# RetNet attention then a gated feed-forward: one ordered load queue for the first chunk and the weights, and a new order around the first feed-forward stage

## The chip, the cores and the metric

The kernel runs on one core of one Trainium2 chip. The metric is the device time of one execution in microseconds (us); smaller is better. The kernel before takes 266.89 us (median of three runs, 266.13 to 267.51).

## The reference

The input is q, k and v of shape [4 batches, 8 heads, 768 positions, 64], and the weights of a feed-forward layer. A recurrent attention with a decay per head is followed by an RMS norm and a gated feed-forward layer:

```python
state = gamma * state + k[t] (outer) v[t]        # one 64x64 state for each batch and head
y[t]  = q[t] @ state / sqrt(64)                  # 768 steps
x     = y, heads side by side                    # 3072 tokens x 512
xn    = x / sqrt(mean(x * x) + 1e-6) * rms_g
out   = (silu(xn @ w_gate) * (xn @ w_val)) @ w_out   # 512 -> 1536 -> 512
```

All inputs and the output are float32; the kernel multiplies in bfloat16.

## The kernel before, in words

The 768 positions are cut into 6 chunks of 128. A chunk of all 4 batches makes 512 tokens, one feed-forward stage. This text calls the feed-forward stages F0 to F5, the batches b0 to b3, and writes q(0,3) for the q tile of chunk 0, batch 3.

Attention of a chunk and batch is done in pieces. `cast` (L138) makes bf16 copies of q and k and scales v by the decay into `vp`. `piece_t` (L158) transposes q and k on TensorE and ScalarE copies the result out of PSUM (L167). `piece_a` (L171) multiplies k and q and VectorE applies the causal mask (L181). `piece_y` (L186) forms y and, for the next chunk, the state update `kv`; VectorE scales y into x (L208), ScalarE sums its squares (L212), GpSimd makes the reciprocal root `rstd` (L230, L233), and ScalarE (chunk 0, L221 and L222) or VectorE and GpSimd (L224, L225) fold kv into the states `st_f` and `st_b`. `piece_n` (L236) normalizes x to xn, and `piece_x` (L248) brings xn transposed into xnT: in chunk 0 by TensorE and VectorE (L255, L256), in later chunks by a DMA transpose on the sync queue (L243).

A feed-forward stage (L278) has 12 slots `gv(n)`, each with 4 matmuls into `g_ps`, 4 into `v_ps`, a Silu on ScalarE (L292) and a product on VectorE (L293), and then 4 slots `down(b)` of 12 matmuls into `o_ps`, whose result ScalarE copies to `o_sb` (L301) and the sync queue stores (L302). The matmul results of the stages rotate through 4 PSUM buffers (`fps`), those of attention through 4 others (`aps`); `o_sb` has 3 buffers, the raw loads 8 of each name.

The order is written out by hand. Ahead of F0, chunk 0's attention runs in the order of a step list (L313). Then the pieces of chunk c+1 are put between the 16 slots of stage c (`PLAN`, `PLAN1` for chunk 1, L264 and L265). Each engine and each queue works in program order.

What is loaded when: at the start the sync queue takes the 12 tiles of chunk 0 (256 KB each, pieces of 256 bytes, float32). GpSimd's queue, which can convert while it moves, takes the gate and value weights in four blocks (`load_w`, W0 to W3, each two transfers) among the steps, and the three blocks of the output weights (`load_wo`, wo0 to wo2) right behind (L315). Chunk 1's loads stand behind the first four Silus of F0 (L328), the broadcast norm weight `g_bc` behind them (L330), and chunk 2's loads at slots 5, 7, 9 and 11 of F0 (L332). Six matmuls that compute nothing needed (`hot`, L319) run ahead of F0.

Of the kernel before, what the change touches and what calls it, by code (L numbers as in the profile page):

```python
# [17 lines left out]
def kernel(  # L18
# [51 lines left out]

    for b in range(B):
        load(0, b)


    ident = const.tile([128, 128], BF16, name="ident")
    make_identity(nc, ident)
    causal = const.tile([128, 128], BF16, name="causal")
    nc.gpsimd.memset(causal, 1.0)
    nc.gpsimd.affine_select(
        out=causal, in_=causal, compare_op=ALU.is_ge, fill=0.0, base=0,  # L80
        pattern=[[1, 128]], channel_multiplier=-1)

    pos_i = const.tile([128, NCH], mybir.dt.int32, name="pos_i")
    nc.gpsimd.iota(pos_i, pattern=[[C, NCH]], base=1, channel_multiplier=1)
    pos_f = const.tile([128, NCH], F32, name="pos_f")
    nc.gpsimd.tensor_copy(pos_f, pos_i)
    lnscale = const.tile([128, 1], F32, name="lnscale")
    nc.gpsimd.memset(lnscale, math.log(scale))
    zero = const.tile([128, 1], F32, name="zero")
    nc.gpsimd.memset(zero, 0.0)  # L90
    vdec = const.tile([128, NCH, H], F32, name="vdec")
    ydec = const.tile([128, NCH, H], F32, name="ydec")
    for h in range(H):
        nc.scalar.activation(vdec[:, :, h], pos_f, AF.Exp, scale=-lng[h], bias=zero)
        nc.scalar.activation(ydec[:, :, h], pos_f, AF.Exp, scale=lng[h], bias=lnscale)
    mhalf = const.tile([128, 1], F32, name="mhalf")
    nc.gpsimd.memset(mhalf, -0.5)

    warm = const.tile([128, 1], F32, name="warm")
    nc.scalar.activation(warm, zero, AF.Silu)  # L100
    g_col = const.tile([128, KS], F32, name="g_col")
# [11 lines left out]
    for b in range(B):  # L113
        nc.gpsimd.memset(st_b[b], 0.0)

# [7 lines left out]
    WB = 384  # L123

    def load_w(i):
        sl = slice(i * WB, (i + 1) * WB)
        nc.gpsimd.dma_start(out=wg_b[:, :, sl], in_=wg_v[:, :, sl])
        nc.gpsimd.dma_start(out=wv_b[:, :, sl], in_=wv_v[:, :, sl])

    def load_wo(i):  # L130
        sl = slice(i * 4, (i + 1) * 4)
        nc.gpsimd.dma_start(out=wo_b[:, sl, :], in_=wo_v[:, sl, :])


    cur = {}
    mark = {}

    def cast(c, b):  # L138
        q_f, k_f, v_f = raw.pop((c, b))
        qb = work.tile([128, DM], BF16, name="qb", bufs=6)  # L140
        kb = work.tile([128, DM], BF16, name="kb", bufs=6)
        vp = work.tile([128, H, D], BF16, name="vp", bufs=6)
        if c == 0:
            nc.vector.tensor_copy(qb, q_f.rearrange("p h d -> p (h d)"))
        else:
            nc.gpsimd.tensor_copy(qb, q_f.rearrange("p h d -> p (h d)"))  # L146
# [39 lines left out]
    def piece_y(c, b):  # L186
# [14 lines left out]
        if c < NCH - 1:  # L201
            kv_ps = aps.tile([128, NHP, 128], F32, name="kv_ps", tag="at")
# [12 lines left out]
        piece_rstd(c, b)  # L215
        if c < NCH - 1:
            for i in range(2):
                r = slice(i * 64, i * 64 + 64)
                kv = kv_ps[r, :, i * 64:i * 64 + 64]
                if c == 0:  # L220
                    nc.scalar.copy(st_b[b][r, :, i * 64:i * 64 + 64], kv)  # L221
                    nc.scalar.copy(st_f[b][r], kv)  # L222
                else:
                    nc.vector.tensor_tensor(out=st_f[b][r], in0=st_f[b][r], in1=kv, op=ALU.add)  # L224
                    nc.gpsimd.tensor_copy(st_b[b][r, :, i * 64:i * 64 + 64], st_f[b][r])  # L225
        d["x"] = x

# [50 lines left out]
    def ffn(c):  # L278
# [4 lines left out]
        def gv(n):  # L283
# [81 lines left out]
```

## Time and profile before

| what | value |
|---|---|
| time, median of three runs | 266.89 us |
| the profiled execution, its own time | 266.61 us |
| its span, first to last instruction | 264.9 us |
| TensorE (PE) busy in the span | 231.2 us |
| VectorE (DVE), ScalarE (ACT), GpSimd (POOL) busy | 124.8, 91.0, 93.9 us |
| mean granted TensorE clock | 0.987 of full speed |
| HBM read, written | 28.58 MB, 6.29 MB |

The profile is that of one execution. A matmul's end is modelled and matmuls overlap, so a stage is best measured from the start of one group to the start of another. POOLq and SPq are the instructions by which GpSimd and the sync engine issue DMAs; q0 is the DMA queue of GpSimd, q1 that of the sync engine. "idle before <-releaser" in a row tells how long the engine stood idle and what ended it.

### The profile page before, as it was taken

To read this page: it belongs to the slowest core of one execution; us is meant where nothing else is said; L and a number is where in the kernel's file an instruction comes from. 1 tells how busy PE (TensorE), PEld (TensorE's weight loads), DVE (VectorE), ACT (ScalarE), POOL (GpSimd) and SP (SyncE) were. 2 spreads that over 40 slices of the span, in tenths; PEclk is the share of its full clock that TensorE was granted. 3 is DMA by queue.
4 is the path that set the end of the run, shared out by engine and by line. 5 is a ranking of instruction groups with operands and counts; after the bars stand their busy time and mean duration, and the time that the engine had idled before them with its cause. 6 is when DMAs were issued, how large, how long until landed. Compare 5 with 4: busy or idle time off the path is not lost.

```text
span 264.9 us, 4103 instructions
## 1 busy us (share of the span) xinstructions
PE 231.2 (87%) x1467; PEld 112.6 (42%) x1494; DVE 124.8 (47%) x208; ACT 91.0 (34%) x187; POOL 93.9 (35%) x177
## 2 busy tenths in 40 slices
PE   1557899996908999999998999999999999999994
PEld 1334344543403454444444444544444444444441
DVE  0547144546421588703689403898126674044400
ACT  8546132424311334314333223323232432333311
POOL 6698301556249022493032690222950111000000
PEclk9999999999986999999999999999999999999999
DMA  8999999999964597944599844599645101300022
GB/s 159 218 172 203 203 199 213 218 200 223 202 216 86 122 190 152 148 139 101 101 216 216 142 143 97 122 227 221 128 120 99 42 20 59 114 27 0 0 82 79
DMA packets 112628, 37.24 MB, mean 141 GB/s; under 512 B 103776, under 2 KB 109408, under 8 KB 112608
## 3 DMA queue, kind: packets, MB, share of 16 engines
q1 hardware_dynamic: 106768, 32.26, 60.5%
q0 software_dynamic: 5840, 4.72, 11.6%
q8 instruction: 12, 0.20, 0.3%
q14 instruction: 8, 0.07, 0.1%
HBM read 28.58 MB, written 6.29 MB: 132 GB/s over the span
## 4 chain that ended last, share of the span: by engine, by line
PE 59%; DVE 12%; DMA 11%; ACT 4%; POOL 4%; SPq 4%; issue 4%; DVEq 0%; ACTq 0%; POOLq 0%
PE o_ps L298 21%; PE g_ps L287 16%; PE v_ps L290 15%; DMA k_f<-in_k_dram 5%; SPq L64 4%; DVE hT L293 4%; DVE am L181 4%; ACT sg L292 2%; DVE xn L241 2%; DMA g_bc<-in_moe_rms_g_dram 2%; DMA v_f<-in_v_dram 2%; PE a_ps L177 2%; DVE x L208 2%; PE y_ps L194 1%; ACT xsq L212 1%
## 5 line engine op out<-in xcount | busy, mean ns | idle before, releaser
L293 DVE TENSOR_TENSOR hT<-sg,v_ps 128x512 bf16<-128x512 bf16 x72 | 49.4, 687 | 94.6 <-PE v_ps L290 83.4
L287 PE MATMUL g_ps<-xnT,wg_b 128*128 128x512 bf16 x275 | 75.2, 390 | 8.7 <-DMA xnT<-xn 7.5
L290 PE MATMUL v_ps<-xnT,wv_b 128*128 128x512 bf16 x282 | 75.2, 386 | 0.5
L292 ACT ACTIVATE sg<-g_ps 128x512 bf16<-128x512 f32 x72 | 42.8, 594 | 71.4 <-PE g_ps L287 68.3
L298 PE MATMUL o_ps<-wo_b,hT 128*128 128x512 bf16 x281 | 63.1, 379 | 0.5 <-issue 0.2
L290 PEld LDWEIGHTS <-wv_b 128*128 128x128 bf16 x288 | 28.6, 99 | 35.3 <-issue 2.2
L287 PEld LDWEIGHTS <-wg_b 128*128 128x128 bf16 x288 | 26.6, 100 | 38.2 <-issue 11.6
L298 PEld LDWEIGHTS <-hT 128*128 128x128 bf16 x288 | 27.8, 98 | 32.3
L230 POOL TENSOR_SCALAR ms<-ssq 128x1 f32<-128x1 f32 x24 | 4.6, 191 | 103.1 <-ACT xsq L212 102.9
L181 DVE TENSOR_TENSOR am<-a_ps,causal 128x512 bf16<-128x512 f32 x48 | 30.8, 683 | 4.5 <-PE a_ps L177 4.5
L212 ACT ACTIVATE xsq<-x 128x512 f32<-128x512 f32 x24 | 15.1, 630 | 45.8 <-DVE x L208 45.6
L301 ACT COPY o_sb<-o_ps 128x512 f32<-128x512 f32 x24 | 14.1, 586 | 44.8 <-PE o_ps L298 37.8
L148 POOL TENSOR_TENSOR vp<-v_f,vdec 128x512 bf16<-128x512 f32 x24 | 25.4, 1060 | 2.5 <-DMA v_f<-in_v_dram 2.4
L241 DVE SCALAR_TENSOR_TENSOR xn<-x,rstd,g_bc 128x512 bf16<-128x512 f32 x20 | 15.5, 776 | 9.9 <-POOL rstd L233 7.8
L208 DVE TENSOR_TENSOR x<-y_ps,ydec 128x512 f32<-128x512 f32 x24 | 16.4, 685 | 7.3 <-PE y_ps L194 5.0
L146 POOL CAST qb<-q_f 128x512 bf16<-128x512 f32 x20 | 12.2, 610 | 14.5 <-DMA q_f<-in_q_dram 14.1
L194 PE MATMUL y_ps<-vp,am 128*128 128x64 bf16 x192 | 13.1, 203 | 4.1 <-DVE am L181 4.0
L147 POOL CAST kb<-k_f 128x512 bf16<-128x512 f32 x24 | 14.7, 612 | 4.9 <-DMA k_f<-in_k_dram 4.9
L194 PEld LDWEIGHTS <-am 128*128 128x128 bf16 x192 | 9.4, 104 | 12.6 <-DVE am L181 11.1
L225 POOL CAST st_b<-st_f 64x256 bf16<-64x256 f32 x32 | 14.0, 439 | 0.9
L233 POOL TENSOR_TENSOR rstd<-ms,mhalf 128x1 f32<-128x1 f32 x24 | 13.2, 552 | 2.0
L224 DVE TENSOR_TENSOR st_f<-st_f,kv_ps 64x256 f32<-64x256 f32 x32 | 13.2, 413 | 0.5
(48 smaller groups left out, 109.2 us busy)
## 6 DMA issues: line engine op xcount, KB each, us to landing
q_f<-in_q_dram SPq DMA_DIRECT2D x24, 256.0 KB, 4.6
k_f<-in_k_dram SPq DMA_DIRECT2D x24, 256.0 KB, 4.9
v_f<-in_v_dram SPq DMA_DIRECT2D x24, 256.0 KB, 5.0
out_dram<-o_sb SPq DMA_DIRECT2D x24, 256.0 KB, 2.1
wg_b<-in_moe_w_gate_dram POOLq DMA_DIRECT2D x4, 384.0 KB, 8.6
wv_b<-in_moe_w_val_dram POOLq DMA_DIRECT2D x4, 384.0 KB, 9.5
wo_b<-in_moe_w_out_dram POOLq DMA_DIRECT2D x3, 512.0 KB, 13.8
xnT<-xn SPq DMA_TRANSPOSE x20, 2.4
```

The costliest lines, as they stand in the source:

```text
L147: nc.gpsimd.tensor_copy(kb, k_f.rearrange("p h d -> p (h d)"))
L148: nc.gpsimd.tensor_tensor(out=vp, in0=v_f, in1=vdec[:, c, :, None].to_broadcast([128, H, D]), op=ALU.mult)
L181: nc.vector.tensor_tensor(out=am[:, i], in0=a_ps[i], in1=causal[:, None, :].to_broadcast([128, NHP, 128]), op=ALU.mult)
L194: nc.tensor.matmul(y_ps[:, h, :], d["am"][:, i, hp, :], d["vp"][:, h, :], start=first, stop=last, skip_group_check=True)
L208: nc.vector.tensor_tensor(out=x, in0=y_ps, in1=ydec[:, c, :, None].to_broadcast([128, H, D]), op=ALU.mult)
L212: nc.scalar.activation(xsq, x.rearrange("p h d -> p (h d)"), AF.Square, accum_out=ssq)
L241: nc.vector.scalar_tensor_tensor(out=xn, in0=x, scalar=d["rstd"], in1=g_bc, op0=ALU.mult, op1=ALU.mult)
L287: nc.tensor.matmul(g_ps, wg_b[:, s, sl], xnT[:, s, :], start=s == 0, stop=s == KS - 1)
L290: nc.tensor.matmul(v_ps, wv_b[:, s, sl], xnT[:, s, :], start=s == 0, stop=s == KS - 1)
L292: mark[c, n] = nc.scalar.activation(sg, g_ps, AF.Silu)
L293: nc.vector.tensor_tensor(out=hT[:, n, :], in0=sg, in1=v_ps, op=ALU.mult)
L298: nc.tensor.matmul(o_ps, hT[:, n, b * C:(b + 1) * C], wo_b[:, n, :], start=n == 0, stop=n == NFF - 1)
```

## The change

- Chunk 0: the tiles of b0 still come by the sync queue. Those of b1 to b3 go into GpSimd's queue (`load0`), q and k converted to bf16 on the way, v as float32; the nine transfers stand ahead of the weights, with the identity and the causal mask made between them. b0's q is cast by VectorE and its k by ScalarE; VectorE scales v (`piece_v`). The decay tables are made by two activations instead of sixteen. `g_col` is loaded by ScalarE's queue.
- Chunk 0's xT of b0 to b2 is emptied by ScalarE in four activations each instead of by VectorE in one. The state copies to `st_f` come after the last steps, those to `st_b` go to GpSimd into slots 0 to 3 of F0; `kv` of chunk 0 is held in `fps`.
- Weights: W1 to W3 stand behind the rstd of b0, b1 and b2 on GpSimd. Output weights are issued at slots 9 and 12 of F0, behind the casts of chunk 1's b2 and b3.
- Chunk 1's loads wait until W1 has landed; chunk 2's loads stand at slot 16, behind g_bc, and wait until wo1 has landed.
- F0 gets 24 slots: `down` goes over all four batches in thirds of the output weights. Chunk 1's pieces are spread over all 24. Chunk 1's xn is transposed by TensorE as in chunk 0, no longer by DMA.

```diff
-    for b in range(B):
-        load(0, b)
+    def load0(b):
+        for name, src in (("qb", q), ("kb", k)):
+            x = work.tile([128, DM], BF16, name=name, bufs=6)
+            nc.gpsimd.dma_start(
+                out=x.rearrange("p (h d) -> p h d", h=H),
+                in_=src[b].rearrange("h (c p) d -> c p h d", p=C)[0])
+            raw0[name, b] = x
+        x = loads.tile([128, H, D], F32, name="v_f")
+        nc.gpsimd.dma_start(out=x, in_=v[b].rearrange("h (c p) d -> c p h d", p=C)[0])
+        raw0["v", b] = x
+    load(0, 0)
...
+    load0(1)
     ident = const.tile([128, 128], BF16, name="ident")
     make_identity(nc, ident)
+    load0(2)
     causal = const.tile([128, 128], BF16, name="causal")
...
+    load0(3)
...
-            for i in range(2):
...
+    def piece_s(b):
+        for i in range(2):
+            r = slice(i * 64, i * 64 + 64)
+            nc.scalar.copy(st_f[b][r], cur[0, b]["kv"][r, :, i * 64:i * 64 + 64])
+    def piece_sb(b):
+        for i in range(2):
+            r = slice(i * 64, i * 64 + 64)
+            nc.gpsimd.tensor_copy(st_b[b][r, :, i * 64:i * 64 + 64], st_f[b][r])
...
+        if c == 0 and b < B - 1:
+            for s in range(KS):
+                nc.scalar.activation(cur[c, "xnT"][:, s, b * C:(b + 1) * C], xt_ps[:, s, :],
+                                     AF.Copy, scale=g_col[:, s:s + 1])
+            return
...
-    PLAN1 = dict(cast=(5, 7, 9, 11), t=(7, 9, 11, 13), a=(8, 10, 12, 14), y=(9, 11, 13, 15), n=(11, 13, 15, 15), x=(13, 15, 15, 15))
+    PLAN1 = dict(cast=(5, 6, 8, 11), t=(7, 9, 11, 17), a=(8, 10, 13, 18), y=(9, 11, 15, 20), n=(11, 13, 17, 22), x=(12, 15, 19, 23))
...
+        if c == 0:
+            for i in range(3):
+                for b in range(B):
+                    slots.append(lambda b=b, i=i: down(b, 4 * i, 4 * i + 4))
...
-    for step in ("C0 T0 C1 G0 A0 T1 Y0 C2 W0 W1 A1 T2 Y1 N0 C3 W2 W3 A2 X0 T3 Y2 N1 A3 X1 Y3 N2 X2").split():
+    for step in ("C0 T0 V0 W0 A0 T1 V1 Y0 W1 A1 T2 V2 N0 Y1 W2 X0 A2 T3 V3 N1 Y2 W3 X1 A3 N2 Y3 X2 S0 S1").split():
         P[step[0]](0, int(step[1]))
-    for i in range(3):
-        load_wo(i)
...
+    for b in range(B):
+        load(1, b, after=landed["w", 1] if b == 0 else None)
+    WS = {9: (0, 1), 12: (2,)}
...
+            if c == 0:
+                for j in WS.get(i, ()):
+                    load_wo(j)
+            f_slot()
             if c == 0 and i < B:
-                load(1, i, after=mark[0, i])
-            if c == 0 and i == 4:
+                piece_sb(i)
+            if c == 0 and i == 16:
                 nc.sync.dma_start(out=g_bc, in_=moe_rms_g.partition_broadcast(128))
-            if c < NCH - 2 and i in (5, 7, 9, 11):
+                for b in range(B):
+                    load(2, b, after=landed["wo", 1])
+            if 0 < c < NCH - 2 and i in (5, 7, 9, 11):
                 load(c + 2, (i - 5) // 2)
```

## Rows read from the trace of the kernel before

**Rows 1.** The profile page: span, and busy time of each engine.
```profile
span 264.9 us, 4103 instructions
PE 231.2 (87%) x1467; PEld 112.6 (42%) x1494; DVE 124.8 (47%) x208; ACT 91.0 (34%) x187; POOL 93.9 (35%) x177
```

**Rows 2.** Busy by stretch: PE, PEld, DVE, ACT, POOL, granted clock, DMA share, GB/s.
```profile
73.00:80.18 7.18, 0.00 (x1) 0.03 (x1) 1.81 (x4) 1.21 (x3) 3.98 (x8) 0.83 0.64 199
80.18:85.00 4.82, 4.82 (x13) 1.77 (x14) 0.69 (x1) 0.60 (x1) 4.82 (x9) 0.55 0.56 109
...
0.00:29.48 29.48, 15.36 (x134) 10.05 (x135) 13.57 (x24) 17.51 (x47) 22.34 (x45) 1.00 1.20 190
29.48:80.18 50.70, 39.52 (x268) 19.60 (x272) 21.87 (x36) 15.71 (x28) 17.77 (x32) 0.98 1.05 207
...
121.19:157.00 35.81, 34.82 (x232) 16.80 (x235) 21.08 (x36) 11.34 (x23) 13.63 (x28) 1.00 0.84 160
```

**Rows 3.** The chain that ended last: start, duration, engine and work.
```profile
32.41 12.91 DMA k_f<-in_k_dram
...
71.67 2.85 DMA out_dram<-o_sb
...
77.73 2.36 DMA xnT<-xn
80.18 1.86 PE g_ps L287 x4
...
87.64 0.86 PE g_ps L287 x4
...
109.37 10.11 PE o_ps L298 x46
```

**Rows 4.** Timeline: where chunk 0's mask falls, and F1's third gate group.
```profile
8.67 1.29 DVE L181 TENSOR_TENSOR am<-a_ps,causal 128x512 bf16<-128x512 f32 x2 [0.47 <-PE a_ps L177]
...
22.02 1.29 DVE L181 TENSOR_TENSOR am<-a_ps,causal 128x512 bf16<-128x512 f32 x2 [0.25 <-PE a_ps L177]
...
85.75 1.03 PE L287 MATMUL g_ps<-xnT,wg_b 128*128 128x512 bf16 x4
```

**Rows 5.** Groups of instructions by form, 0 to 30 us: busy, mean ns.
```profile
L181 DVE TENSOR_TENSOR am<-a_ps,causal 128x512 bf16<-128x512 f32 x8 | 5.1, 684 | 0.9 <-PE a_ps L177 0.9
L148 POOL TENSOR_TENSOR vp<-v_f,vdec 128x512 bf16<-128x512 f32 x4 | 4.2, 1040 | 1.5 <-DMA v_f<-in_v_dram 1.4
...
L127 POOL DMA_DIRECT2D wg_b<-in_moe_w_gate_dram x4 | 3.2, 797 | 0.0
L222 ACT COPY st_f<-kv_ps 64x256 f32<-64x256 f32 x8 | 2.9, 365 | 0.0
...
L208 DVE TENSOR_TENSOR x<-y_ps,ydec 128x512 f32<-128x512 f32 x4 | 2.8, 692 | 5.1 <-PE y_ps L194 5.0
...
L212 ACT ACTIVATE xsq<-x 128x512 f32<-128x512 f32 x4 | 2.5, 630 | 1.9 <-DVE x L208 1.6
...
L94 ACT ACTIVATE vdec<-pos_f,zero 128x6 f32<-128x6 f32 x8 | 2.3, 291 | 0.3 <-POOL zero L90 0.3
```

**Rows 6.** DMA queues, 15.5 to 16 us: packets, MB, share of 16 engines.
```profile
q1 hardware_dynamic: 433, 0.11, 134.9%
```

**Rows 7.** DMA queues, 18 to 19 us.
```profile
q0 software_dynamic: 266, 0.20, 131.9%
```

**Rows 8.** DMA queues, 34 to 38 us.
```profile
q0 software_dynamic: 705, 0.70, 104.5%
q1 hardware_dynamic: 367, 0.09, 17.7%
```

**Rows 9.** Timeline of ScalarE, 57 to 84 us: the copies of F0's output.
```profile
69.04 0.59 ACT L301 COPY o_sb<-o_ps 128x512 f32<-128x512 f32 x1 [0.85 <-PE o_ps L298]
74.62 0.59 ACT L301 COPY o_sb<-o_ps 128x512 f32<-128x512 f32 x1 [5.00 <-DMA out_dram<-o_sb]
```

**Rows 10.** Timeline of the sync queue, 44 to 80 us: chunk 2's last load.
```profile
68.78 1.01 SPq L64 DMA_DIRECT2D v_f<-in_v_dram  x1
```

More of the change, by code (lines that the diff above doesn't have):

```diff
@@ L69, in load @@
         raw[c, b] = t
-    for b in range(B):
-        load(0, b)
+    raw0 = {}
+    def load0(b):
[9 more added lines that the diff above has]
+    load(0, 0)
+    g_col = const.tile([128, KS], F32, name="g_col")
+    with nc.allow_non_contiguous_dma(reason="one column per 128 entries"):
+        nc.scalar.dma_start(out=g_col, in_=moe_rms_g.rearrange("(s p) -> p s", p=128))
+    pos_i = const.tile([128, NCH], mybir.dt.int32, name="pos_i")
+    nc.gpsimd.iota(pos_i, pattern=[[C, NCH]], base=1, channel_multiplier=1)
+    lngs = const.tile([128, H], F32, name="lngs")
+    for h in range(H):
+        nc.vector.memset(lngs[:, h:h + 1], lng[h])
+    lnscale = const.tile([128, 1], F32, name="lnscale")
+    nc.vector.memset(lnscale, math.log(scale))
+    zero = const.tile([128, 1], F32, name="zero")
+    nc.vector.memset(zero, 0.0)
+    pos_f = const.tile([128, NCH], F32, name="pos_f")
+    nc.vector.tensor_copy(pos_f, pos_i)
+    darg = const.tile([128, NCH, H], F32, name="darg")
+    nc.vector.tensor_tensor(
+        out=darg, in0=pos_f[:, :, None].to_broadcast([128, NCH, H]),
+        in1=lngs[:, None, :].to_broadcast([128, NCH, H]), op=ALU.mult)
+    vdec = const.tile([128, NCH, H], F32, name="vdec")
+    ydec = const.tile([128, NCH, H], F32, name="ydec")
+    nc.scalar.activation(vdec, darg, AF.Exp, scale=-1.0, bias=zero)
+    nc.scalar.activation(ydec, darg, AF.Exp, scale=1.0, bias=lnscale)
+    warm = const.tile([128, 1], F32, name="warm")
+    nc.scalar.activation(warm, zero, AF.Silu)
+    mhalf = const.tile([128, 1], F32, name="mhalf")
+    nc.vector.memset(mhalf, -0.5)
+    load0(1)
     ident = const.tile([128, 128], BF16, name="ident")
     make_identity(nc, ident)
+    load0(2)
     causal = const.tile([128, 128], BF16, name="causal")
@@ L81 @@
         pattern=[[1, 128]], channel_multiplier=-1)
[L83 to L101, printed above, removed]
+    load0(3)
     g_bc = const.tile([128, DM], F32, name="g_bc")
-    def load_g():
-        with nc.allow_non_contiguous_dma(reason="one column per 128 entries"):
-            nc.gpsimd.dma_start(out=g_col, in_=moe_rms_g.rearrange("(s p) -> p s", p=128))
     st_f = [const.tile([128, NHP, D], F32, name=f"st_f{b}") for b in range(B)]
@@ L113 @@
     for b in range(B):
-        nc.gpsimd.memset(st_b[b], 0.0)
+        nc.vector.memset(st_b[b], 0.0)
     wg_b = const.tile([128, KS, DFF], BF16, name="wg_b")
@@ L123 @@
     WB = 384
+    landed = {}
     def load_w(i):
@@ L127, in load_w, with piece_c, piece_v @@
         nc.gpsimd.dma_start(out=wg_b[:, :, sl], in_=wg_v[:, :, sl])
-        nc.gpsimd.dma_start(out=wv_b[:, :, sl], in_=wv_v[:, :, sl])
+        landed["w", i] = nc.gpsimd.dma_start(out=wv_b[:, :, sl], in_=wv_v[:, :, sl])
     def load_wo(i):
         sl = slice(i * 4, (i + 1) * 4)
-        nc.gpsimd.dma_start(out=wo_b[:, sl, :], in_=wo_v[:, sl, :])
+        landed["wo", i] = nc.gpsimd.dma_start(out=wo_b[:, sl, :], in_=wo_v[:, sl, :])
     cur = {}
-    mark = {}
+    def piece_c(b):
+        q_f, k_f, v_f = raw.pop((0, b))
+        for name, x in (("qb", q_f), ("kb", k_f)):
+            raw0[name, b] = work.tile([128, DM], BF16, name=name, bufs=6)
+            copy = nc.vector.tensor_copy if name == "qb" else nc.scalar.copy
+            copy(raw0[name, b], x.rearrange("p h d -> p (h d)"))
+        raw0["v", b] = v_f
+    def piece_v(b):
+        vp = work.tile([128, H, D], BF16, name="vp", bufs=6)
+        nc.vector.tensor_tensor(
+            out=vp, in0=raw0["v", b], in1=vdec[:, 0, :, None].to_broadcast([128, H, D]), op=ALU.mult)
+        cur[0, b]["vp"] = vp
     def cast(c, b):
@@ L142, in cast @@
         vp = work.tile([128, H, D], BF16, name="vp", bufs=6)
[L143 to L146, printed above, removed]
+        nc.gpsimd.tensor_copy(qb, q_f.rearrange("p h d -> p (h d)"))
         nc.gpsimd.tensor_copy(kb, k_f.rearrange("p h d -> p (h d)"))
@@ L160, in piece_t @@
             return
+        if c == 0:
+            cur[c, b] = dict(qb=raw0["qb", b], kb=raw0["kb", b])
         d = cur[c, b]
@@ L201, in piece_y @@
         if c < NCH - 1:
-            kv_ps = aps.tile([128, NHP, 128], F32, name="kv_ps", tag="at")
+            pool, tag = (fps, "ff") if c == 0 else (aps, "at")
+            kv_ps = pool.tile([128, NHP, 128], F32, name="kv_ps", tag=tag)
             for hp in range(NHP):
@@ L215, in piece_y @@
         piece_rstd(c, b)
-        if c < NCH - 1:
+        d["x"] = x
+        if c == 0:
+            d["kv"] = kv_ps
+        elif c < NCH - 1:
             for i in range(2):
@@ L219, in piece_y @@
                 kv = kv_ps[r, :, i * 64:i * 64 + 64]
[L220 to L226, printed above, removed]
+                nc.vector.tensor_tensor(out=st_f[b][r], in0=st_f[b][r], in1=kv, op=ALU.add)
+                nc.gpsimd.tensor_copy(st_b[b][r, :, i * 64:i * 64 + 64], st_f[b][r])
[6 more added lines that the diff above has]
+            r = slice(i * 64, i * 64 + 64)
+            nc.gpsimd.tensor_copy(st_b[b][r, :, i * 64:i * 64 + 64], st_f[b][r])
     def piece_rstd(c, b):
@@ L248, in piece_x @@
     def piece_x(c, b):
-        d = cur.pop((c, b))
-        if c > 0:
+        d = cur[c, b] if c == 0 else cur.pop((c, b))
+        if c > 1:
             return
@@ L264 @@
     PLAN = dict(cast=(0, 1, 2, 3), t=(1, 3, 5, 7), a=(4, 6, 8, 10), y=(5, 7, 9, 11), n=(7, 9, 11, 13), x=(8, 10, 12, 14))
-    PLAN1 = dict(cast=(5, 7, 9, 11), t=(7, 9, 11, 13), a=(8, 10, 12, 14), y=(9, 11, 13, 15), n=(11, 13, 15, 15), x=(13, 15, 15, 15))
+    PLAN1 = dict(cast=(5, 6, 8, 11), t=(7, 9, 11, 17), a=(8, 10, 13, 18), y=(9, 11, 15, 20), n=(11, 13, 17, 22), x=(12, 15, 19, 23))
     def attention(c):
-        s = [[] for _ in range(16)]
+        s = [[] for _ in range(24 if c == 1 else 16)]
         s[0].append(lambda: begin(c))
@@ L291, in gv, with down @@
             sg = ffw.tile([128, GT], BF16, name="sg")
-            mark[c, n] = nc.scalar.activation(sg, g_ps, AF.Silu)
+            nc.scalar.activation(sg, g_ps, AF.Silu)
             nc.vector.tensor_tensor(out=hT[:, n, :], in0=sg, in1=v_ps, op=ALU.mult)
-        def down(b):
-            o_ps = fps.tile([128, DM], F32, name="o_ps", tag="ff")
-            for n in range(NFF):
+        o_t = {}
+        def down(b, n0=0, n1=NFF):
+            if n0 == 0:
+                o_t[b] = fps.tile([128, DM], F32, name="o_ps", tag="ff")
+            o_ps = o_t[b]
+            for n in range(n0, n1):
                 nc.tensor.matmul(o_ps, hT[:, n, b * C:(b + 1) * C], wo_b[:, n, :],
                                  start=n == 0, stop=n == NFF - 1)
+            if n1 < NFF:
+                return
             o_sb = ffw.tile([128, DM], F32, name="o_sb")
@@ L305, in ffn @@
             slots.append(lambda n=n: gv(n))
-        for b in range(B):
-            slots.append(lambda b=b: down(b))
+        if c == 0:
+            for i in range(3):
+                for b in range(B):
+                    slots.append(lambda b=b, i=i: down(b, 4 * i, 4 * i + 4))
+        else:
+            for b in range(B):
+                slots.append(lambda b=b: down(b))
         return slots
     begin(0)
-    P = dict(C=cast, T=piece_t, A=piece_a, Y=piece_y, N=piece_n, X=piece_x, W=lambda c, i: load_w(i), G=lambda c, i: load_g())
-    for step in ("C0 T0 C1 G0 A0 T1 Y0 C2 W0 W1 A1 T2 Y1 N0 C3 W2 W3 A2 X0 T3 Y2 N1 A3 X1 Y3 N2 X2").split():
+    P = dict(C=lambda c, b: piece_c(b), V=lambda c, b: piece_v(b), S=lambda c, b: piece_s(b),
+             T=piece_t, A=piece_a, Y=piece_y, N=piece_n, X=piece_x, W=lambda c, i: load_w(i))
+    for step in ("C0 T0 V0 W0 A0 T1 V1 Y0 W1 A1 T2 V2 N0 Y1 W2 X0 A2 T3 V3 N1 Y2 W3 X1 A3 N2 Y3 X2 S0 S1").split():
         P[step[0]](0, int(step[1]))
-    for i in range(3):
-        load_wo(i)
-    hot = fps.tile([128, GT], F32, name="hot", tag="ff")
+    hot = aps.tile([128, GT], F32, name="hot", tag="at")
     for i in range(6):
-        nc.tensor.matmul(hot, ident, st_b[0].rearrange("p a b -> p (a b)"), start=True, stop=True)
+        nc.tensor.matmul(hot, ident, cur[0, 3]["qT"].rearrange("p a b -> p (a b)"), start=True, stop=True)
+    piece_s(2)
+    piece_s(3)
     piece_n(0, 3)
     piece_x(0, 3)
+    for b in range(B):
+        load(1, b, after=landed["w", 1] if b == 0 else None)
+    WS = {9: (0, 1), 12: (2,)}
     for c in range(NCH):
@@ L324 @@
         a_slots = attention(c + 1) if c + 1 < NCH else [[] for _ in range(16)]
-        for i in range(16):
-            f_slots[i]()
+        for i, f_slot in enumerate(f_slots):
+            if c == 0:
+                for j in WS.get(i, ()):
+                    load_wo(j)
+            f_slot()
             if c == 0 and i < B:
-                load(1, i, after=mark[0, i])
-            if c == 0 and i == 4:
+                piece_sb(i)
+            if c == 0 and i == 16:
                 nc.sync.dma_start(out=g_bc, in_=moe_rms_g.partition_broadcast(128))
-            if c < NCH - 2 and i in (5, 7, 9, 11):
+                for b in range(B):
+                    load(2, b, after=landed["wo", 1])
+            if 0 < c < NCH - 2 and i in (5, 7, 9, 11):
                 load(c + 2, (i - 5) // 2)
```

2 lines of the change are left out of this document (1 added, 1 removed).

## The prediction

> **What bounds the kernel now.** I read the page first: TensorE is busy for 231.2 of 264.9 us [rows 1], so what there is to win is its idle time and its slow time. The stretches show where these lie [rows 2]. The two before F1 are poor: ahead of F0 (29.48 us) TensorE is busy for 15.36 us, and from F0's first matmul to F1's (50.70 us) for 39.52. A later stage is full (34.82 of 35.81). Between 73.00 and 80.18 TensorE does nothing, and the granted clock falls: 0.83 in that stretch, 0.55 in the next 4.82 us, where F1 starts near the lower of its two levels (1.2 of 2.4 GHz). The third gate group of F1 starts at 85.75 [rows 4]. That is the place from which I count: everything behind it is the same code on the same data.
>
> Then the chain of waits says why F1 starts at 80.18 [rows 3]. A k tile of chunk 1 needs 12.91 us to land, because the output weights stream beside it; near the end a store of F0's output holds the chain for 2.85 us; and the last xnT comes by a DMA transpose of 2.36 us. ScalarE's timeline shows that store from the other side [rows 9]: the fourth copy into `o_sb` needs the first store's buffer back and waits 5.00 us for it, until 74.62. That store is issued behind chunk 2's last load, of 68.78 [rows 3, 10]. So before 75 us it is the line of transfers that paces F0: 12 tiles, four weight blocks, three output blocks, 12 tiles, g_bc, 12 tiles.
>
> **The transfers.** A 256 KB tile on the sync queue: 433 packets of 256 bytes in half a microsecond [rows 6], so 1024 take 1.2 us, 12 tiles 14.4 us. The weights alone: 266 packets in a microsecond [rows 7], 1024 packets a block, so 3.9 us, four blocks 15.4. The output weights: 705 packets in 4 us [rows 8], 512 a block, so 2.9 us, 8.7 for three; beside them the sync queue gets 367 packets in 4 us, 0.36 of a tile. All that precedes F0's first store: 3 x 14.4 + 15.4 + 8.7 + 1.2 (g_bc, 256 KB, taken as a tile) = 68.5 us, which with about 2 us ahead of the first byte is where the trace has that store issued (71.67). The change reorders these transfers and removes none. I take the sum as unchanged, and that decides the forecast.
>
> **Chunk 0.** GpSimd loses b0 to b3's casts and `vp` (1.04 us each [rows 5]) and gets nine transfers of 1024 pieces. No row shows one; a weight transfer of 512 pieces costs 0.80 us of GpSimd [rows 5]. The bounds are 0.8 (no dependence on pieces) and 1.6 (proportional); I take 1.1, nearer the row. GpSimd then reaches the end of the causal mask after 0.7 + 3.3 + 0.5 + 3.3 + 0.5 = 8.3 us (identity and mask at 0.5 each), and b0's masking can start at 8.7, as before (8.67 [rows 4]). Per batch VectorE then does vp 0.69 (priced as x), mask 1.37, x 0.69, xn about 0.5: 3.25 us. ScalarE loses sixteen decay activations (0.29 each) and the eight state casts, and gets 12 activations of 128x128: between 0.29 and 0.63 by the smallest and the full row [rows 5]; at 0.3 that is 1.2 us a batch, beside 1.0 of qkT and 0.8 of squares, so it stays under VectorE. With rstd behind the two issues of a weight block I take 3.5 us a batch: the last masking starts at 8.7 + 3 x 3.5 = 19.2. Before it started at 22.02 and F0 followed 7.46 us later, of which some 1.1 us was `piece_x` of b3 standing behind the `hot` matmuls; these now run while xn is awaited. F0 then starts at 19.2 + 6.4 = 25.6, 3.9 earlier. The loads allow it: the twelfth tile lands by 2 + 14.4 + 0.6 = 17. The bounds are 23.5 (0.8 us an issue) and 29 (1.6, whose last tile is issued at 16).
>
> The state copies cost nothing at first: the eight of `st_f` (0.365 each, 2.9 us of ScalarE) run while VectorE and GpSimd finish b3; F0's first matmuls need the first two kv buffers back, some 1 us ahead of need. Without that cover it would be 1 to 1.5 us. `st_b` is first read at slot 9.
>
> **F0.** Matmul work of this stretch is 39.52 us [rows 2], plus 16 transposes of chunk 1's xn at 0.1 each: 41.1. If nothing else stalls, F0's slots end at 25.6 + 41.1 = 66.7. Chunk 1's tiles now come first: W1 has landed at about 26, W2 and W3 take until about 35 while the sync queue gets under half a tile in 4 us, and the remaining 11 tiles need 13 us, to 48. b0's three are there at 38 for slot 7 (about 41), b1's at 42 for slot 9, b2's at 45 for slot 11. The price is paid by wo: issued behind b2's cast at 46, wo0 lands about 50 and wo1 54, for slots 12 (53) and 16 (57). wo2 stands behind b3's cast, whose v is starved beside wo0 and wo1 and lands at 55 to 58; so wo2 lands at 60 to 65, for slot 20 (62). A stall of 0 to 3 us there is likely. At the end `piece_y` of b3 at slot 20 is followed by x 0.69, squares 0.8, rstd 0.75, xn 0.75, four transposes and xnT 0.69, about 4.7 us with handovers, of which three slots (12 x 0.22 = 2.6 us [rows 3]) cover a part: 2.1 us more. F1 can start at 69 to 72.
>
> **The gate that is late next.** F0's four output banks are the same four buffers that F1's first groups need: g(0), v(0) and g(1) go, and v(1) needs the fourth bank, so the fourth `o_sb` copy, so the first store, so chunk 2's twelve loads ahead of it on the sync queue. The transfers' sum is unchanged, so that copy starts at 74.6 as before [rows 9]: 74.6 + 0.6 (copy) + 0.86 (v(1) [rows 3]) = 76.1 for the third gate group, against 85.75. This also hides a start of F1 anywhere up to 72.6 (g0, v0, g1 are 2.6 us ahead of 75.2). TensorE idles for some 2 to 4 us there in place of 7.18; if the clock falls again, it costs at most what 4.82 us at 0.55 cost now, about 2.2 us.
>
> The sum: 266.61 (the profiled execution, span 264.9 and 1.7 around it) - (85.75 - 76.1 = 9.65) = **257.0 us**. It lies 0.28 under the median of the runs, 266.89, which I leave out. Own range 255 to 260.
>
> **Rivals.** *One: the gate falls away too* (254). The nine tiles on GpSimd's queue may cost the engines less: weights move 266 x 1536 bytes a microsecond, 1.85 times the rate of the 256-byte tiles. At 0.36 us less a tile the store is back 3.2 us earlier and TensorE's own work decides: 69.4 + 4 x 0.86 = 72.9, 12.9 us won, 253.7. Against it: no row shows small pieces moved faster. The Trainium skill ("DMA: Bandwidth & Descriptors", Why small descriptors are slow) says that a 256-byte piece pays 3 cycles on 8 and that putting pieces together into a packet saves them; by that the nine tiles would give back 9 x 0.33 = 2.9 us, an estimate, and nearly this rival.
>
> *Two: b0 is starved* (261). Its tiles stay on the sync queue while GpSimd's queue fills. Beside wo the sync queue got one packet for two [rows 8], and a k tile needed 12.91 us [rows 3]. If k(0,0) does too, it lands at 14 instead of 6, b0 comes 8 us later; the others are then all there and follow at 3.25: F0 at 32.7, its end and tail at 75.9, the third gate group at about 79.5 to 80. W1, behind b0's rstd, is issued at 23 with the queue empty since 19, which moves the store as much: 80.1, 5.7 us won. Twice as deep a hole leaves no change. For it: the order of the queue. Against it: until 12 us GpSimd issues hardly faster than the engines move. The Trainium skill (same page, Queues, rings and completion order) has a DMA engine drain a whole packet of several pieces from one queue before it turns to the next, which speaks for this rival; the two-for-one of rows 8 agrees.
>
> *Three: slower* (281). Small converting pieces in GpSimd's queue cost as much as its large ones. A weight packet takes 16/266 = 60 ns of an engine, a sync packet 16/866 = 18.5 ns. At 60 ns a tile needs 64 x 60 = 3.8 us, nine tiles 34.6 instead of 10.7: 23.9 us more in front of everything, 281. It decides from 9.65 us on, that is from 35 ns a packet. Against it: beside large packets the sync queue's small ones pass at about their own price. But no row shows a small converting piece.
>
> **Chances.** Forecast 0.52, rival one 0.17, rival two 0.16, the deep hole (no change) 0.05, rival three 0.10. Faster by over 0.5%, which is about what a measurement here can tell from none: 0.52 + 0.17 + 0.16 = 0.85; same 0.05; slower 0.10. The range 251 to 264 takes in the forecast and rivals one and two with their bounds (1.6 us an issue, a fallen clock) and leaves out rival three and the hole.
>
> **What would show it.** F0's first matmul at 23.5 to 29; q, k and v of b3 landed by 18; GpSimd's nine issues at 0.8 to 1.6 us; v(1,3) landing between 50 and 58 and wo2 by 65; the fourth `o_sb` copy waiting for a store until 73 to 76; F1's third gate group at 75 to 79; and a distance from there to the end as before. The prediction is wrong if the nine tiles' packets take over 30 ns, if b0's k lands after 9 us, or if TensorE waits for wo2 beyond 66.

## The result, and the profile after

The changed kernel takes 257.8 us (median, 256.02 to 258.41) against 266.51 for the kernel before on the same chip: ratio 0.9662, 95% interval 0.9599 to 0.9725. A second set of runs gave 0.9611 (0.9578 to 0.9645). The forecast was 257.0, range 251 to 264.

The profiled execution took 256.02 us, the shortest of the four. Its page, as in [rows 1]:

```profile
span 254.3 us, 4122 instructions
PE 228.2 (90%) x1483; PEld 112.4 (44%) x1510; DVE 127.7 (50%) x227; ACT 90.0 (35%) x178; POOL 96.1 (38%) x177
```

Then the stretches, with the columns of [rows 2]: ahead of F0, F0 to F1, F1's first four groups, and the rest.

```profile
0.00:25.67 25.67, 14.87 (x133) 10.02 (x135) 14.90 (x39) 15.62 (x36) 21.14 (x38) 1.00 1.36 179
25.67:69.81 44.14, 38.86 (x283) 19.98 (x288) 23.43 (x40) 16.32 (x30) 20.13 (x38) 1.00 1.09 198
69.81:74.85 5.04, 3.57 (x15) 1.58 (x17) 0.38 (x1) 1.49 (x3) 5.04 (x8) 1.00 0.90 239
...
74.85:254.30 179.45, 170.87 (x1053) 80.85 (x1071) 89.03 (x148) 56.60 (x111) 49.83 (x96) 1.00 0.60 119
```

The same last stretch of the kernel before, from the third gate group of F1 to the end:

```profile
85.75:264.90 179.15, 170.78 (x1052) 80.85 (x1071) 88.72 (x147) 56.55 (x110) 48.17 (x93) 1.00 0.56 115
```

So the whole gain lies ahead of that group: 85.75 - 74.85 = 10.9 us, of which 0.3 are lost behind it. Where in the span it lies: F0 starts 3.8 us earlier, F0 to F1 takes 44.14 us in place of 50.70 (6.6), and F1's first four groups take 5.04 in place of 5.57 (0.5).

The timeline shows what is late now. TensorE waits 2.66 us for the third block of the output weights, F1 starts at 69.81, and its second value group waits 1.42 us for the fourth `o_sb` copy, which has waited 5.37 us for a store:

```profile
25.67 1.02 PE L336 MATMUL g_ps<-xnT,wg_b 128*128 128x512 bf16 x4 [0.88 <-ACT st_f L264]
...
63.93 1.02 PE L351 MATMUL o_ps<-wo_b,hT 128*128 128x512 bf16 x4 [2.66 <-DMA wo_b<-in_moe_w_out_dram]
...
69.81 1.04 PE L336 MATMUL g_ps<-xnT,wg_b 128*128 128x512 bf16 x4 [0.79 <-DVE xnT L304]
...
73.36 0.59 ACT L356 COPY o_sb<-o_ps 128x512 f32<-128x512 f32 x1 [5.37 <-DMA out_dram<-o_sb]
...
73.99 1.02 PE L339 MATMUL v_ps<-xnT,wv_b 128*128 128x512 bf16 x4 [1.42 <-ACT o_sb L356]
...
74.85 1.03 PE L336 MATMUL g_ps<-xnT,wg_b 128*128 128x512 bf16 x4
```

### The profile page after: what moved, and what is told of

Same layout as the page of the kernel before. It is cut to its first block, busy times and chain, and to the rows that moved or that the text cites. A ratio compares the mean times of both kernels' runs of the same rounds, so it can differ in the third digit from the quotient of the medians.

```text
span 254.3 us, 4122 instructions
## 1 busy us (share of the span) xinstructions
PE 228.2 (90%) x1483; PEld 112.4 (44%) x1510; DVE 127.7 (50%) x227; ACT 90.0 (35%) x178; POOL 96.1 (38%) x177
## 3 DMA queue, kind: packets, MB, share of 16 engines
q0 software_dynamic: 12288, 6.29, 18.4%
## 4 chain that ended last, share of the span: by engine, by line
PE 63%; DVE 13%; POOL 6%; ACT 6%; issue 5%; DMA 5%; SPq 0%; ACTq 0%; DVEq 0%; POOLq 0%
PE o_ps L351 21%; PE v_ps L339 19%; PE g_ps L336 17%; DVE am L215 5%; DVE hT L342 4%; DMA wo_b<-in_moe_w_out_dram 3%; DVE x L243 2%; ACT sg L341 2%; PE y_ps L228 2%; ACT xsq L247 2%; DMA out_dram<-o_sb 2%; PE a_ps L211 2%; DVE xn L284 1%; POOL v_f L83 1%; POOL kb L78 1%
## 5 line engine op out<-in xcount | busy, mean ns | idle before, releaser
L339 PE MATMUL v_ps<-xnT,wv_b 128*128 128x512 bf16 x282 | 73.4, 379 | 1.9 <-ACT o_sb L356 1.4
L336 PE MATMUL g_ps<-xnT,wg_b 128*128 128x512 bf16 x275 | 72.8, 380 | 2.1 <-ACT st_f L264 0.9
L351 PE MATMUL o_ps<-wo_b,hT 128*128 128x512 bf16 x281 | 63.8, 379 | 3.2 <-DMA wo_b<-in_moe_w_out_dram 2.7
L336 PEld LDWEIGHTS <-wg_b 128*128 128x128 bf16 x288 | 26.0, 98 | 29.8 <-issue 1.0
L180 POOL TENSOR_TENSOR vp<-v_f,vdec 128x512 bf16<-128x512 f32 x20 | 20.7, 1036 | 2.1 <-DMA v_f<-in_v_dram 2.1
L284 DVE SCALAR_TENSOR_TENSOR xn<-x,rstd,g_bc 128x512 bf16<-128x512 f32 x16 | 12.2, 765 | 4.9 <-POOL rstd L276 4.9
L179 POOL CAST kb<-k_f 128x512 bf16<-128x512 f32 x20 | 12.1, 607 | 1.3 <-DMA k_f<-in_k_dram 1.2
```

What stands on the lines that cost most here:

```text
L180: nc.gpsimd.tensor_tensor(out=vp, in0=v_f, in1=vdec[:, c, :, None].to_broadcast([128, H, D]), op=ALU.mult)
L336: nc.tensor.matmul(g_ps, wg_b[:, s, sl], xnT[:, s, :], start=s == 0, stop=s == KS - 1)
L339: nc.tensor.matmul(v_ps, wv_b[:, s, sl], xnT[:, s, :], start=s == 0, stop=s == KS - 1)
```

## The experiments

The first four ran on one chip, the others in two later sets; across sets the ratios to the kernel before are compared. "Gate" below is the store gate of the prediction; the "place" is the start of F1's third gate group. From that place to the end the twelve experiments' profiles have 179.1 to 179.5 us, but for one of 180.2 that starts the stretch at half pace, so the place tells the time.

**The changed kernel again.**

> The changed kernel itself, on the chip of the three that follow, so that they can be set against it: 256 to 258.5 us. Both theories expect the third gate group of F1 within 0.5 us of 74.85.

257.59 us (255.4 to 258.12), ratio 0.9611 (0.9578 to 0.9645). Its profiled execution is one of the longer ones: the place is at 76.77, not within 0.5 of 74.85. Between 65 and 70 us, behind a wait of 2.64 us for the third output block, the granted clock was 0.66, where the execution shown above kept 1.00. From the end of that wait to F1 took 6.96 us for 5.88. But TensorE still waits 1.14 us for the fourth copy:

```profile
65.00:70.00 5.00, 4.95 (x29) 2.74 (x29) 1.58 (x4) 1.90 (x4) 0.93 (x3) 0.66 0.88 193
...
75.28 0.59 ACT L356 COPY o_sb<-o_ps 128x512 f32<-128x512 f32 x1 [4.52 <-DMA out_dram<-o_sb]
...
75.91 1.02 PE L339 MATMUL v_ps<-xnT,wv_b 128*128 128x512 bf16 x4 [1.14 <-ACT o_sb L356]
```

So the store gate sets the place here too, 1.9 us later than in the first profile, and the fallen clock is hidden behind it. Chunk 2's first load is issued 1.1 us later (54.87 for 53.73) and its last 2.2 later (70.16 for 67.91). Why the loads run late in this execution stays open.

**Four buffers for o_sb.**

```diff
-            o_sb = ffw.tile([128, DM], F32, name="o_sb")
+            o_sb = ffw.tile([128, DM], F32, name="o_sb", bufs=4)
```

> One buffer more for o_sb (four), nothing else. Theory: F1's third gate group is held by the fourth o_sb copy, which waits for the first store, which stands behind chunk 2's loads on the sync queue. Then that wait (5.37 us on ScalarE) disappears, the third gate group starts 4 x 0.86 = 3.5 us after F1's first matmul, about 73.3, and the kernel is 1.6 us faster than the changed one (0.6%). Rival, that TensorE's own work with its wait for the third block of the output weights sets the place: no change beyond 0.3 us.

255.06 us, ratio 0.9533 (0.9513 to 0.9554): 2.5 us less than the changed kernel on that chip. The fourth copy no longer waits for a store and the place is where the theory put it, 73.34, 1.5 us earlier than in the first profile of the changed kernel and 3.4 earlier than in the second:

```profile
68.33 0.59 ACT L356 COPY o_sb<-o_ps 128x512 f32<-128x512 f32 x1 [0.28 <-PE o_ps L351]
...
73.34 1.03 PE L336 MATMUL g_ps<-xnT,wg_b 128*128 128x512 bf16 x4
```

The gate is shown: one buffer, no load, store or matmul moved.

**The third output block with the other two.**

```diff
-    WS = {9: (0, 1), 12: (2,)}
+    WS = {9: (0, 1, 2)}
```

> The third block of the output weights is issued at slot 9 with the other two, no longer behind b3's cast. Both expect TensorE's wait of 2.66 us for it to go and F1 to start near 67. Theory (store gate): the fourth o_sb copy still waits for a store until 71.5 to 73.5, so of the 2.66 us only the hole in the transfers between 53 and 57 us is won: 0 to 1.8 us. Rival (the wait for that block set the place): the third gate group moves by all of 2.7 us, to about 72.2.

255.2 us, ratio 0.9539 (0.9513 to 0.9564), 2.4 less. The wait of 2.66 is gone, F1 starts at 66.79, and the gate holds it as the theory said: 6.41 us for the store, 2.45 on TensorE, which then runs four matmuls at half pace (1.87).

```profile
71.37 0.59 ACT L356 COPY o_sb<-o_ps 128x512 f32<-128x512 f32 x1 [6.41 <-DMA out_dram<-o_sb]
...
72.00 1.87 PE L339 MATMUL v_ps<-xnT,wv_b 128*128 128x512 bf16 x4 [2.45 <-ACT o_sb L356]
73.67 1.74 PE L336 MATMUL g_ps<-xnT,wg_b 128*128 128x512 bf16 x4
```

By the medians the gain is larger than the theory's 0 to 1.8. The store comes 2 us earlier (copy at 71.37 for 73.36), and the queues fit that: GpSimd's moves 373 packets of the block from 53.5 to 56 us, where it moves none in the changed kernel, and the block no longer runs beside chunk 2's loads until 64. The place (73.67, about 72.9 had that group run at full pace, not the 72.2 of the rival) is held by the gate; so in the changed kernel both the gate and the wait stood in the way.

**Both.**

> Both edits. Theory: the gate and the wait are both gone, F1 starts near 67.2 and its third gate group at about 70.6, 4.2 us earlier than in the changed kernel, 253.6 us or 1.6% less. Rival: as with the output block alone, 2.7 us. A third outcome, that chunk 2's tiles come too late for F1 then: a wait for its casts near slot 4 of F1 and less than 2 us won.

251.91 us, ratio 0.9428 (0.9404 to 0.9452): 5.7 us less than the changed kernel, the fastest version of this study. F1 starts at 66.64, its second value group waits for nothing, and the place is at 70.10 (theory: about 70.6):

```profile
65.09 0.59 ACT L356 COPY o_sb<-o_ps 128x512 f32<-128x512 f32 x1 [0.28 <-PE o_ps L351]
...
70.10 1.03 PE L336 MATMUL g_ps<-xnT,wg_b 128*128 128x512 bf16 x4
```

**The output weights early, as before the change.**

```diff
+    for i in range(3):
+        load_wo(i)
     hot = aps.tile([128, GT], F32, name="hot", tag="at")
-    WS = {9: (0, 1), 12: (2,)}
+    WS = {}
```

> The three blocks of the output weights are issued right behind W3 as in the kernel before; all else as changed. Theory of the order: chunk 1's tiles starve beside them again, a k tile of chunk 1 takes over 10 us to land, the first TensorE transposes of chunk 1 (slot 7) wait 3 to 7 us, F1 starts at 71 to 74, and the kernel is 1 to 3 us slower than the changed one. Rival, that the gain comes from the early start of F0 and the 24 slots and not from the order of loads: within 0.5 us of the changed kernel.

254.64 us, ratio 0.9538 (0.9497 to 0.9579): 0.0073 x 267 = 1.9 us less than the changed kernel, with intervals that only touch and a place (72.91) ahead of both its profiles. On the same chip all its executions (254.16 to 255.86) are shorter than all those of the two kernels below that time like the changed one ("F0 held back", "VectorE empties xT again", 256.41 to 258.32). Both theories fail. Chunk 1 does starve: GpSimd waits 5.97 us for k(1,0), issued at 24.14 and there at 40.44. But chunk 2's loads now follow chunk 1's without a gap, the store is back at 70.8, and TensorE, which waits only 1.5 us for the late casts and not at all for the third output block, reaches the place at 72.91:

```profile
40.44 0.61 POOL L179 CAST kb<-k_f 128x512 bf16<-128x512 f32 x1 [5.97 <-DMA k_f<-in_k_dram]
...
70.82 0.58 ACT L356 COPY o_sb<-o_ps 128x512 f32<-128x512 f32 x1 [3.20 <-DMA out_dram<-o_sb]
...
72.91 1.03 PE L336 MATMUL g_ps<-xnT,wg_b 128*128 128x512 bf16 x4
```

So as the change made it, moving the output weights back cost time.

**Chunk 0 on the sync queue again.**

```diff
-    load(0, 0)
+    for b in range(B):
+        load(0, b)
-    load0(1)
...
-    for step in ("C0 T0 V0 W0 A0 T1 V1 Y0 W1 A1 T2 V2 N0 Y1 W2 X0 A2 T3 V3 N1 Y2 W3 X1 A3 N2 Y3 X2 S0 S1").split():
+    for step in ("C0 T0 V0 W0 A0 C1 T1 V1 Y0 W1 A1 C2 T2 V2 N0 Y1 W2 X0 A2 C3 T3 V3 N1 Y2 W3 X1 A3 N2 Y3 X2 S0 S1").split():
```

> Chunk 0's twelve tiles all on the sync queue as float32 again, cast by VectorE (q) and ScalarE (k); all else as changed. Theory (the gate decides, the start of F0 doesn't): VectorE and ScalarE get 0.43 and 0.62 us a batch more, F0 starts 1 to 3 us later than 25.67, the wait for the third output block shrinks by as much, and the time is within 0.8 us of the changed kernel. Rival (F0's early start is the gain): it is slower by the whole delay, 1.5 to 3 us.

262.62 us, ratio 0.9822 (0.9783 to 0.9861), 0.0211 x 267 = 5.6 us more than the changed kernel. F0 starts 6.6 us later, more than theory or rival had, since the edit had a second effect that I had not foreseen: with GpSimd's queue empty W0 is issued at 2.02 us, and q(0,1), which the kernel before casts at 7.78, is there only at 12.69.

```profile
2.02 0.96 POOL L147 DMA_DIRECT2D wg_b<-in_moe_w_gate_dram  x1
...
12.69 0.43 DVE L162 CAST qb<-q_f 128x512 bf16<-128x512 f32 x1 [1.82 <-DMA q_f<-in_q_dram]
...
32.22 1.24 PE L334 MATMUL g_ps<-xnT,wg_b 128*128 128x512 bf16 x4 [0.88 <-DVE xnT L302]
```

**The same with the weights behind the tiles.**

```diff
+        if i == 0:
+            tc.add_manual_dep(first.ins, landed["load", 0, 2].ins.name, SYNC_DEP, reason="transfer order")
...
+    for step in ("C0 T0 C1 V0 W0 A0 T1 V1 Y0 C2 W1 A1 T2 V2 N0 Y1 C3 W2 X0 A2 T3 V3 N1 Y2 W3 X1 A3 N2 Y3 X2 S0 S1").split():
```

> Chunk 0's twelve tiles on the sync queue as float32 again, but now W0 waits on GpSimd until v(0,2) has landed, and the casts stand a step earlier than in the other kernel with chunk 0 on the sync queue, which lost 5 us while W0 streamed beside the tiles. Theory (order): it is the order, tiles before weights, that makes chunk 0 quick, not the queue: F0 starts at 26.5 to 28.5 instead of 32.2 and the time is within 1 us of the changed kernel, 257 to 258.6. Rival (queue): converting on the way in GpSimd's queue is itself what saves the time: F0 starts at 30 or later and the time stays above 260.

259.5 us, ratio 0.973 (0.9687 to 0.9772), between the two theories; F0 starts at 28.87. Against the kernel above, the order of tiles and weights (with the casts a step earlier) gave 0.0092 x 267 = 2.5 us. What is left to the changed kernel is 0.0119 x 267 = 3.2 us. F0's start alone doesn't explain it: with F0 at 28.12 the kernel of the next experiment loses next to nothing. In this profile the third output block is issued at 59.24, TensorE waits 3.92 us for it and then runs at half pace (four matmuls in 1.86 us), which puts F1 at 75.77. How much of the 3.2 us is the casts that GpSimd's queue takes off VectorE and ScalarE, how much the quicker tiles and how much this later wait was not separated.

```profile
28.87 1.02 PE L336 MATMUL g_ps<-xnT,wg_b 128*128 128x512 bf16 x4 [0.88 <-DVE xnT L304]
...
68.06 1.86 PE L351 MATMUL o_ps<-wo_b,hT 128*128 128x512 bf16 x4 [3.92 <-DMA wo_b<-in_moe_w_out_dram]
...
79.23 1.03 PE L336 MATMUL g_ps<-xnT,wg_b 128*128 128x512 bf16 x4
```

**F0 held back.**

```diff
-    for i in range(6):
+    for i in range(20):
         nc.tensor.matmul(hot, ident, cur[0, 3]["qT"].rearrange("p a b -> p (a b)"), start=True, stop=True)
```

> 20 in place of 6 idle matmuls ahead of F0, nothing else: F0 starts 2 to 4 us later. Theory (slack): 2.66 us of wait for the third output block and 1.42 us at F1's second value group stand behind F0, so a delay up to about 2.7 us is taken up whole and the time is within 0.5 us of the changed kernel; at 4 us 1.3 are lost at most. Rival: the time grows by the delay, 2 to 4 us.

257.27 us, ratio 0.9626 (0.959 to 0.9662): 0.4 us more than the changed kernel, within the noise, with F0 2.5 us later. So the slack is there, but not where the theory had it: the wait for the third output block only goes from 2.66 to 2.36 us, because the block's issue moves along (58.81 for 56.35), standing behind a cast that stands behind F0's own work. What shrinks is the wait at the gate, 1.42 to 0.47. The place, 76.04, lies between the two profiles of the changed kernel.

```profile
28.12 1.02 PE L336 MATMUL g_ps<-xnT,wg_b 128*128 128x512 bf16 x4 [0.88 <-DVE xnT L304]
...
66.07 1.02 PE L351 MATMUL o_ps<-wo_b,hT 128*128 128x512 bf16 x4 [2.36 <-DMA wo_b<-in_moe_w_out_dram]
...
75.18 1.02 PE L339 MATMUL v_ps<-xnT,wv_b 128*128 128x512 bf16 x4 [0.47 <-ACT o_sb L356]
```

**VectorE empties xT again.**

```diff
-        if c == 0 and b < B - 1:
+        if False:
```

> Chunk 0's xT of b0 to b2 is emptied by VectorE in one instruction again, nothing else. VectorE has 0.69 us a batch more: F0 starts 0.5 to 2 us later. Theory (slack): no change within 0.5 us. Rival (VectorE's chain of chunk 0 carries to the end): 0.5 to 2 us slower.

256.6 us, ratio 0.9611 (0.9569 to 0.9652): no change. It doesn't need the slack either, F0 starts at 25.38: this part of the change is worth nothing that these runs can tell.

```profile
25.38 1.02 PE L336 MATMUL g_ps<-xnT,wg_b 128*128 128x512 bf16 x4 [0.88 <-DVE xnT L304]
```

**Output weights early and four buffers.** The edits of "The output weights early" and "Four buffers for o_sb" together.

> Output weights right behind W3 and four o_sb buffers. With the store gate out of the way in both, this against the kernel with four buffers and all three blocks at slot 9 (251.9 us) is the order of chunk 1 and the output weights alone. Theory: chunk 1's starved tiles hold F1's start at 69.4 as with three buffers (there the fourth copy came at 70.8, before its bank was needed), so no gain over 254.6 us, and the order chunk 1 first is worth 2.7 us. Rival: 252, the order is worth nothing.

254.33 us, ratio 0.9546 (0.9528 to 0.9565). The fourth buffer adds nothing where the store comes early, and TensorE waits 2.7 us for chunk 1's casts (two waits, the longest 2.0). Against 0.9428 with chunk 1 first: that order is worth 0.0118 x 267 = 3.2 us, 2.6 by the place (72.73 for 70.10), once nothing else holds F1. The theory had 2.7.

```profile
PE qk_ps L199 <- POOL kb L179: 2.7, 2, 2.0
```

**The kernel before with four buffers.**

> The kernel before with four o_sb buffers, nothing else. There the fourth copy held ScalarE for 5.00 us, and with it the squares of b3 behind it (from 73.2 to 75.1). Theory: F1 starts 1.9 us earlier, and the idle stretch ahead of it is shorter by as much; 1.5 to 3 us less than before, 264 to 265.5. Rival, that the xnT transposes on the sync queue behind chunk 2's loads set F1's start anyway: within 0.5 us of before.

266.14 us, ratio 0.9993 (0.9967 to 1.0018): the rival is right. The squares of b3 come 2.6 us earlier, but F1 still waits 7.6 us for xnT, whose last two DMA transposes stand on the sync queue behind chunk 2's loads and the stores:

```profile
72.46 0.63 ACT L212 ACTIVATE xsq<-x 128x512 f32<-128x512 f32 x1 [0.66 <-DVE x L208]
...
75.68 2.54 SPq L243 DMA_TRANSPOSE xnT<-xn  x2
...
79.47 1.87 PE L287 MATMUL g_ps<-xnT,wg_b 128*128 128x512 bf16 x4 [7.61 <-DMA xnT<-xn]
```

**The fastest version with one idle matmul.** Range 1 in place of 6, on top of both edits.

> Four o_sb buffers, all three output blocks at slot 9, and one idle matmul ahead of F0 instead of six. The changed kernel starts F0 at the full pace (four matmuls in 1.02 us), the kernel before at half (1.88). Theory: the idle matmuls keep the pace up; with one, F0's first 8 to 16 matmuls run at half pace, which costs 1 to 2 us now that no slack takes it up: 253 to 254 against 251.9. Rival: the transposes and products of chunk 0 suffice, no change.

253.35 us, ratio 0.9516 (0.9489 to 0.9542), 0.0088 x 267 = 2.3 us more than with six; the place is at 71.89, 1.8 us later. F0's first eight matmuls and most of the third group run at half pace, and the granted clock is 0.50 from 20 to 28.4 us:

```profile
25.00 1.86 PE L336 MATMUL g_ps<-xnT,wg_b 128*128 128x512 bf16 x4 [0.88 <-DVE xnT L304]
...
28.37 1.52 PE L336 MATMUL g_ps<-xnT,wg_b 128*128 128x512 bf16 x4
...
30.58 1.03 PE L336 MATMUL g_ps<-xnT,wg_b 128*128 128x512 bf16 x4
```

So the six don't keep the pace up here, they bring it back. In the kernel with both edits they run at half pace themselves, at a granted clock of 0.50, and F0 then starts at full pace (four matmuls in 1.02 us at 25.20). In the kernel before, six run too and F0 still starts at half pace; why is not shown. Four of the six:

```profile
22.01 1.91 PE L378 MATMUL hot<-qkT,ident 128*128 128x512 bf16 x4 [0.22 <-issue]
```

## Why the prediction was right, step by step

**The sum.** Forecast 257.0, measured 257.8. The step that decides, that F1's third gate group moves by the gate and that all behind it stays, is borne out: 10.9 us at the place in the first profile and 9.0 in the second for the 9.65 forecast, and one added buffer moves it. At the gate TensorE idles 1.42 and 1.14 us, for the 2 to 4 forecast. How the 10.9 us divide among the parts of the change is shown only for chunk 0's loads, xT and the order of the output weights. That the DMA transposes of chunk 1's xn held F1 in the kernel before is read from its 7.61 us of wait with four buffers; no run put them, or the 16 slots, back.

**Chunk 0.** F0 was put at 25.6 and started at 25.67 (25.61 in the second profile). GpSimd issues a tile of 1024 pieces in 0.9 us (1.10 for the first; taken: 1.1), k(0,0) is there at 5.65, so b0 isn't starved (rival two), the mask is done at 8.7 and the last masking starts at 19.31 (19.2):

```profile
2.50 0.89 POOL L78 DMA_DIRECT2D kb<-in_k_dram  x1
...
5.65 0.62 ACT L164 CAST kb<-k_f 128x512 bf16<-128x512 f32 x1 [0.99 <-DMA k_f<-in_k_dram]
...
8.75 1.29 DVE L215 TENSOR_TENSOR am<-a_ps,causal 128x512 bf16<-128x512 f32 x2 [0.23 <-PE a_ps L211]
...
19.31 1.29 DVE L215 TENSOR_TENSOR am<-a_ps,causal 128x512 bf16<-128x512 f32 x2 [0.64 <-PE a_ps L211]
```

But the start decided little: 2.5 us more of it cost nothing that the runs can tell.

**The transfers.** "The sum unchanged" held to 1.3 us (the copy at 73.36, in the second profile at 75.28, for 74.6), by two errors of opposite sign; that they nearly cancel is luck. The DMA queues by stretch (packets, MB, share of 16 engines), 16 to 18, 46 to 53 and 53 to 57 us:

```profile
q0 software_dynamic: 544, 0.41, 131.4%
...
q0 software_dynamic: 1019, 1.02, 96.6%
q1 hardware_dynamic: 66, 0.11, 6.4%
...
q1 hardware_dynamic: 1987, 0.50, 57.7%
```

The weights flow at their full rate (0.41 MB in 2 us) from 16 us, 2 us earlier than in [rows 7]: the twelve tiles are through at about 14 us, for 16.5 before, part of rival one. The Trainium skill's sentence on pieces put together ("DMA: Bandwidth & Descriptors", Why small descriptors are slow) agrees in direction: q0 has 12288 packets on the page in place of 5840, 6448 more for 9216 pieces. No run separates this from the halved bytes that the converted q and k write. Then the sync queue stands all but empty from 46 to 53, because chunk 2's loads wait for the second output block, and runs half full to 57. I had the wait in the text, but not the hole. With the output weights early the hole is gone and the store is back at 70.8.

**The output weights.** The wait at slot 20 came as forecast (63.93 for 60 to 65, 2.66 us for 0 to 3), by another mechanism. v(1,3) was not starved: chunk 1 was there by about 47. The third block stood behind b3's cast in GpSimd's program order, and that cast stood behind b1's rstd and states, at slot 11, which TensorE reached at 50:

```profile
52.72 0.55 POOL L276 TENSOR_TENSOR rstd<-ms,mhalf 128x1 f32<-128x1 f32 x1
53.23 0.93 POOL L259 CAST st_b<-st_f 64x256 bf16<-64x256 f32 x2
...
54.22 0.61 POOL L178 CAST qb<-q_f 128x512 bf16<-128x512 f32 x1
...
56.35 0.83 POOL L154 DMA_DIRECT2D wo_b<-in_moe_w_out_dram  x1
```

**F0's work.** I took 41.1 us from the kernel before, where F0's first two groups run at half pace (1.86 and 1.91 us). Here they start at full pace, 1.9 us less work (with the third group), which the waits took up.

**Rivals.** Three (a converting packet at a large one's price) is excluded by chunk 0's times. Two's mechanism exists, in the place where W0 was issued beside the tiles: q(0,1) came 5 us late. The Trainium skill's rule behind it (same page, Queues, rings and completion order) agrees in direction with that run. In the changed kernel it cost little: v(0,0) is used at 7.83 us, against 6.68 before, and the first masking starts at 8.75 for 8.67.

**What I misjudged.** That the order chunk 1 before the output weights is what helps: in this kernel it cost about 2 us net (by intervals that only touch), since it opened the hole and the wait. It pays, 3.2 us, only once both limits behind it are gone.

## What to carry to other kernels

Follow a transfer order to the last use of its queue: a store that a buffer needs back, behind a block of prefetches, can hold the next stage, and one more buffer removes it. It gave nothing in the kernel before, where the stage also waited for transposes on the same queue. Where two limits end within 2 us of each other, remove both before judging either: alone they gave 2.5 and 2.4 us, together 5.7, and the order of the loads changed from a cost of 2 us to a gain of 3. When a load is placed behind a compute step on an issuing engine, count everything that stands ahead of that step in its program order: such a load moves along with the stage that it is for.

## What the runs showed of the hardware

TensorE's pace and the granted clock did not always agree. In the kernel before, four matmuls took 1.86 us at 29.48, in a stretch whose clock column shows 1.00. In the second profile of the changed kernel four idle matmuls took 1.91 us, with 1.00 in the column from 22 to 24 us:

```profile
22.40 1.91 PE L378 MATMUL hot<-qkT,ident 128*128 128x512 bf16 x4 [0.22 <-issue]
```

In the kernel with both edits the same four took the same 1.91 us with 0.50 in the column (22 to 23.5 us), and with one idle matmul F0's first four took 1.86 us with 0.50; there column and pace agree. Behind six idle matmuls F0's first four took 1.02 us in the changed kernel. A wait of 2.45 us was followed by four matmuls in 1.87 us, one of 2.64 by four in 1.38, one of 2.66 by four in 1.02. And an issue on GpSimd of 1024 pieces costs 0.9 us, hardly more than the 0.8 of one of 512.
